# Four products every half unit for the second layer's groups of the last two column blocks, and a new order of GpSimd's steps

## The chip, the cores and the metric

The kernel runs on one core of a Trainium2 chip. A core has five engines that run side by side, each through its own list of instructions in order: TensorE (PE, matrix products into PSUM banks), VectorE (DVE), ScalarE (ACT), GpSimd (POOL, which works in SBUF only) and SyncE (SP), which here issues all DMAs. They wait for each other through semaphores. The metric is the device time of one execution in microseconds (us). Before the change the median of three runs is 1492.81 us (1492.2 to 1493.12).

## The reference

The input is `x`, 2048 rows of 512 in float32. After a layer norm, attention and a two-layer perceptron work on the same normalised rows, and both are added to `x`:

```python
xn = _layernorm(x, axis=-1)
return x + _A_ref(xn, A_wqkv, A_wo) + _B_ref(xn, B_w1, B_b1, B_w2, B_b2)

# _A_ref: 32 heads of 16
scores = jnp.einsum("bhqd,bhkd->bhqk", q, k) * (Dh ** -0.5)
p = _softmax(scores, axis=-1)
o = jnp.einsum("bhqk,bhkd->bhqd", p, v)      # then @ wo

# _B_ref: 512 -> 1792 -> 512
h = _gelu(jnp.einsum("bsd,df->bsf", x, w1) + b1)
return jnp.einsum("bsf,fd->bsd", h, w2) + b2
```

## The kernel before, in words

**Split numbers.** Most products are made from float16 halves. A float32 operand is split into a high part and a low part, and a product of two operands is made of three products (high-high, high-low, low-high; `PAIRS`). The splitting of weights, of projected queries and keys and of gelu outputs is GpSimd's main work: scale or copy to float16 (`hi`), subtract (`lo`).

**Units.** Attention sets the beat. Heads are taken four at a time (8 groups), queries in 4 column blocks of 512, keys in 16 blocks of 128: 8 x 4 x 16 = 512 units. `unit` (one call per unit) writes the instructions of one unit. For four heads it makes scores for the row maxima (`s_half`, PSUM banks "S", reduced by VectorE at L348), and 19 units later (`LEAD`) the transposed scores (`e_half`, banks "T"), whose exponential ScalarE takes (L395); one or two units after that come the products with the values (`v_half`, bank "V"). A unit has two halves (`a` = 0 and 1). In each half the V products use one half of the array's rows and the dense work (below) the other half. A column block of a group of heads is called `t` (32 of them, 16 units each). After its last unit, `v_end` copies the sums and, over the next ten or so units, small steps divide by the softmax sum and store the result `ot` to DRAM; then `t` is `ready`.

**The dense stream.** All other products are groups of a generator: `group(gen)` takes the next one, `dense` writes its products. A group has an order of products, a PSUM bank, a `finish` (the eviction and what follows), perhaps a condition `ready` for each product, and a `pace`: how many products each half of a unit may write. `FAST` is 4 in every unit, `MEAN` 3 and 4 in turn, `SLOW` 3. If a group ends in the middle of a unit's allowance, the rest of the allowance is not used by the next group; if the next product isn't ready, or the generator has nothing (it yields None), the unit passes without. Three generators follow one another:

- `rest`: the last projections of values, queries and keys, 12 products a group, FAST. `project`'s `finish` copies the sum to `pf` on ScalarE (L584, two buffers) and gives two GpSimd steps to `pooled` that write `stg` (L585, L586, three buffers); the DMA to `qk_d` is issued some units later. Beside it `prepare` splits 16 chunks of the layers' weights (`split_steps`, L1173 to L1175), one every 4.5 units. This stage ends when both are through.
- `mlp`: four column blocks `b`. In each, 14 groups of 12 products for the hidden columns (SLOW and FAST in turn; eviction `hh`, L1287; gelu on GpSimd and ScalarE), and then four groups of 42 products for the second layer (MEAN; eviction `yt`, L1310). A product of the second layer needs the gelu of its hidden column to be written out (`done`).
- `tail`: the output projection, 16 groups of 12 products for column blocks 2, 0, 3, 1 in this order. Blocks 2 and 3 begin without the last group of heads, whose part comes in short groups (`o_end`, L526; from `ol` for block 2, from the last `ot` for block 3). A block's groups come only when its read (`read_o`, L1335) has been issued; that is done by `when`, for blocks with `ready`, at places 4 to 13 of every 16 units or after the last score unit. After the last score unit the "S" banks take a second group at two products a half (`spare`), and evictions go to VectorE (L1344); before, to ScalarE and GpSimd (`ys`, L1351). What is left after the last unit is written by `land` and `drain`.

**Order on the queues.** The order on each engine is that in which the Python code calls the instructions; nothing is reordered. Two lists defer work: `later(n, fn)` runs `fn` n units on (bulk transfers wait in a `lane`, one a unit), and `pooled(...)` appends GpSimd steps, each with an assumed time; `run_steps` takes steps from the front at the end of each unit, up to 2500 ns of them.

**Weight chunks.** `chunk` asks for a chunk's two half loads through the lane (`half`, L791); `fetch` asks for one chunk more than the one wanted. `prepare` gives a chunk's split to `pooled` as soon as both halves have been issued (`got[1]`), the split before is through the list, and all values are projected (`got`, `chunk` and the wait at L1207).

Of the kernel before, what the change touches and what calls it, by code (L numbers as in the profile page):

```python
# [24 lines left out]
NT = S // P  # L25
# [7 lines left out]
FAST, MEAN, SLOW = (4, 4), (3, 4), (3, 3)  # L33
# [20 lines left out]
def layer_kernel(ctx: ExitStack, tc: tile.TileContext, x, wqkv, wo, w1, b1, w2, b2, out):  # L54
# [225 lines left out]
    def later(n, fn, local=False, bulk=False):  # L280
        queue.append((slot[0] + n, fn, local, bulk))
# [14 lines left out]

    steps, room = [], [0]

    def pooled(*todo):
        steps.extend(todo)  # L300

    def run_steps(all_of_them=False):
        room[0] = min(room[0], 0) + POOL_NS
        while steps and (room[0] > 0 or all_of_them):
            ns, fn = steps.pop(0)
            room[0] -= ns
            fn()

# [258 lines left out]
    def project(m, w, sb, wh, bank):  # L567

        prods = [lambda c=c, i=i, j=j: (wh[:, w, i, c, :], xt[:, j, c, sb * QB:(sb + 1) * QB])
                 for c in range(NC) for i, j in PAIRS]  # L570

        dst = qk_d[w, m * P:(m + 1) * P, :, sb * QB:(sb + 1) * QB]

        def finish(pj):
            def put():
                nc.sync.dma_start(dst[:, w:w + 2, :], stg)
                nc.sync.dma_start(dst[:, 2 - 2 * w, :], stg[:, 0])
                if not m:
                    later(2, lambda: stacks(0, w, [sb]), True)

            stg = ph.tile([P, 2, QB], F16, name="stg", bufs=3)
            given("act", 600)
            pf = ph.tile([P, QB], F32, name="pf", bufs=2)
            nc.scalar.activation(pf, pj, AF.Copy)  # L584
            hi = lambda: nc.gpsimd.tensor_scalar(stg[:, 0], pf, 1.0, 0.0, op0=ALU.mult, op1=ALU.add)  # L585
            lo = lambda: nc.gpsimd.tensor_tensor(stg[:, 1], pf, stg[:, 0], op=ALU.subtract)  # L586
            later(1, lambda: pooled((620, hi), (1160, lo), (0, lambda: later(2, put, True))), True)

        return Group(prods, bank, finish)

# [22 lines left out]
    pos, spent, cur = [0], [False], [None]  # L613
    v_done = []
# [162 lines left out]
    with ExitStack() as st1:  # L777
# [6 lines left out]
        def chunk(src):  # L784
            wf = ph.tile([P, 4 * W], F32, name="wch", bufs=3)
            v = wf.rearrange("p (a b) -> p a b", b=src.shape[2])
            n = src.shape[1] // 2
            got = [v, 0]

            def half(r):  # L790
                nc.sync.dma_start(v[:, r], src[:, r])  # L791
                got[1] += 1

            for a in range(2):
                later(2, lambda r=slice(n * a, n * a + n): half(r), True, True)
            return got
# [232 lines left out]
        for w in (1, 0):  # L1029
            wf, hi, lo, i1 = ("wq", 0, w), wqh[:, w, 0], wqh[:, w, 1], inv0[:, w:w + 1]  # L1030
# [18 lines left out]
        for i in range(2):  # L1049
            hi, lo = (wvh[j][:, :, i * W:(i + 1) * W] for j in range(2))  # L1050
# [5 lines left out]
            else:  # L1056
                b = add("POOL", 1240, lambda key=key: nc.gpsimd.tensor_scalar(
                    tl[key], tl[key], inv_v[:, 0:1], 0.0, op0=ALU.mult, op1=ALU.add), [h])
# [34 lines left out]
        def turn_m():  # L1093
            tl[mkey] = sb_tile(mkey)
            for k in range(2):
# [7 lines left out]
        put = [add("SP", 600, lambda k=k: nc.sync.dma_start(m_d[0, :, :, 64 * k:64 * k + 64], mhl[32 * k:32 * k + 16]), [a], size=4)  # L1103
               for k in range(2)]
# [73 lines left out]
        def prepare():  # L1178
            am = am_all
            nc.vector.tensor_reduce(am[:, 7:8], b1_s, axis=AX.X, op=ALU.max, apply_absolute_value=True)  # L1180
            nc.vector.tensor_reduce(am[:, 8:9], amx[:, 7:14], axis=AX.X, op=ALU.max)
            nc.vector.tensor_reduce(am[:, 9:10], amx[:, 14:16], axis=AX.X, op=ALU.max)
            box = []
            yield
            yield from scales(am, 14, sbank, box)
            inv, fac = box
            fac1.append(fac)
            inv1.append(inv)
            by_slots(split_qk(1, wfs[1], inv, ready_w))
            nc.vector.tensor_tensor(sexp[:, 1:3], fac[:, 10:14:2], fac[:, 11:14:2], op=ALU.mult)  # L1190
            nc.vector.tensor_scalar_mul(sexp[:, 1:3], sexp[:, 1:3], DH ** -0.5)
            nc.vector.tensor_copy(sexp[:, 3:4], sexp[:, 2:3])
            yield

            nc.vector.reduce_max(gs[:, 0:1], fac[:, 0:8], axis=AX.X)
            nc.gpsimd.tensor_tensor(gs[:, 3:4], fac_v[0][:, 0:1], fac[:, 9:10], op=ALU.mult)
            yield
            nc.vector.reciprocal(gs[:, 1:2], gs[:, 0:1])
            nc.gpsimd.tensor_tensor(gs[:, 2:3], gs[:, 0:1], fac[:, 8:9], op=ALU.mult)
            yield  # L1200
            nc.vector.tensor_scalar_mul(gs[:, 1:2], gs[:, 1:2], 0.5)
            ended = [True]
            for n in range(16):
                while pos[0] < LEAD + WFROM + WSTEP * n:
                    yield
                got = fetch(NM + n)
                while not ended[0] or len(v_done) < NT or got[1] < 2:  # L1207
                    yield
                v = got[0]
                ended[0] = False  # L1210

                def then(wh=None, n=n):
                    ended[0] = True
                    later(2, lambda: put(wh, n), True)

                def put(wh, n):
                    for a in range(2):
                        if n < 7:
                            later(0, lambda a=a: nc.sync.dma_start(w1_d[n, :, a], wh[:, a]), True, True)
                        elif n < 14:  # L1220
                            later(0, lambda a=a: nc.sync.dma_start(w2_d[:, :, 2 * n - 14 + a], wh[:, :, a]), True, True)

                if n >= 14:
                    i = 2 * (n - 14)
                    split_steps(wo_s[:, 0, i:i + 2, :], wo_s[:, 1, i:i + 2, :], v, inv[:, 9:10], then)
                    continue
                if n < 7:

                    wh = ph.tile([P, 2, 2, NC, P], F16, name="wsp", bufs=3)
                    split_steps(wh[:, :, 0], wh[:, :, 1], v.rearrange("p c (a n) -> p a c n", n=P), inv[:, n:n + 1],  # L1230
                                lambda wh=wh, then=then: then(wh))
                else:
                    wh = ph.tile([P, 2, 2, D], F16, name="wsp", bufs=3)
                    split_steps(wh[:, 0], wh[:, 1], v, inv[:, 8:9], lambda wh=wh, then=then: then(wh))
            while not ended[0]:
                yield
# [9 lines left out]
    def mlp():  # L1246
# [3 lines left out]
        done = set()  # L1250
# [21 lines left out]
        for b in range(NQB):  # L1272
# [20 lines left out]
            for q in range(4):  # L1293
# [14 lines left out]
                def store(yp, xa=xa, t=t):  # L1308
# [6 lines left out]

                yield Group([lambda f=f, i=i, j=j, q=q, g=g: (g[:, i, f, q * P:(q + 1) * P], w2_s[:, j, f, :])
                             for f in range(NF) for i, j in PAIRS], dbank, store,
                            lambda n, b=b: (b, n // 3) in done, pace=MEAN)

    def when(t, fn, n=1):  # L1320

# [148 lines left out]
```

## Time and profile before

| | |
|---|---|
| median of three runs | 1492.81 us |
| the profiled execution's own time | 1491.85 us |
| its span, first to last instruction | 1489.9 us |
| TensorE busy, granted clock | 1471.6 us, 0.998 |
| VectorE, ScalarE, GpSimd busy | 1376.0, 1264.9, 660.9 us |
| row maxima (L348), exponentials (L395) | 1296.7 and 1111.4 us |
| last second-layer eviction `yt` | at 1378.3 us |

A row of the profile names the line, the engine, the operation, the tiles (written <- read) with their shapes, a count, and behind the bar the busy time, the mean of one in ns, and the idle time of the engine just before these instructions with what ended it. Timeline rows begin with start and duration in us; square brackets hold the idle time before and its releaser. A row with "x4" is four merged instructions. A busy TensorE isn't TensorE at its peak, since its instructions overlap: four quarter-width instructions (64*32) and both row halves run at the same time. Releasers are inferred.

### The profile page before, as it was taken

To read this page: it belongs to the slowest core of one execution; us is meant where nothing else is said; L and a number is where in the kernel's file an instruction comes from. 1 tells how busy PE (TensorE), PEld (TensorE's weight loads), DVE (VectorE), ACT (ScalarE), POOL (GpSimd) and SP (SyncE) were. 2 spreads that over 40 slices of the span, in tenths; PEclk is the share of its full clock that TensorE was granted. 3 is DMA by queue.
4 is the path that set the end of the run, shared out by engine and by line. 5 is a ranking of instruction groups with operands and counts; after the bars stand their busy time and mean duration, and the time that the engine had idled before them with its cause. 6 is when DMAs were issued, how large, how long until landed. Compare 5 with 4: busy or idle time off the path is not lost.

```text
span 1489.9 us, 88034 instructions
## 1 busy us (share of the span) xinstructions
PE 1471.6 (99%) x40140; PEld 815.1 (55%) x40140; DVE 1376.0 (92%) x2307; ACT 1264.9 (85%) x2365; POOL 660.9 (44%) x671
## 2 busy tenths in 40 slices
PE   8999999999999999999999999999999999999998
PEld 4445555555555555555555555555555555555553
DVE  7899989999999999999999999999999999999913
ACT  5868888888999888899988889998888999888873
POOL 3202667663777311377831137782113777211200
PEclk9999999999999999999999999999999999999999
DMA  7732565553224210211112111121113110111342
GB/s 213 233 104 67 157 194 171 173 177 115 78 70 114 65 37 23 75 54 41 43 44 86 29 46 42 50 71 56 30 30 93 38 43 23 48 53 33 110 131 91
DMA packets 112621, 124.80 MB, mean 84 GB/s; under 512 B 22908, under 2 KB 84220, under 8 KB 112248
## 3 DMA queue, kind: packets, MB, share of 16 engines
q1 hardware_dynamic: 112248, 119.18, 26.6%
q8 instruction: 313, 5.13, 1.5%
q14 instruction: 60, 0.49, 0.1%
HBM read 81.66 MB, written 37.34 MB: 80 GB/s over the span
## 4 chain that ended last, share of the span: by engine, by line
PE 88%; DVE 8%; DMA 2%; ACT 1%; issue 1%; SPq 1%; POOL 0%; DVEq 0%; POOLq 0%; ACTq 0%
PE pV L168 26%; PE pD L168 24%; PE pS L168 18%; PE pT L168 18%; DVE mt L348 6%; PE pT L971 1%; DMA wq<-in_A_wqkv_dram 1%; DVE ac L1344 0%; PE pD L971 0%; DMA qk_d<-stg 0%; DMA kst<-qk_d 0%; DMA qst<-qk_d 0%; DMA m_d<-mhl 0%; ACT xs L924 0%; DVE mneg L364 0%
## 5 line engine op out<-in xcount | busy, mean ns | idle before, releaser
L348 DVE TENSOR_REDUCE mt<-pS 128x1 f32<-128x512 f32 x2029 | 1296.7, 684 | 44.9 <-PE pS L168 26.0
L395 ACT ACTIVATE pe<-pT 128x512 f32<-128x512 f32 x2048 | 1111.4, 599 | 170.2 <-PE pS L168 68.8
L168 PE MATMUL pV<-pe,vv 64*32 64x512 f32 x8192 | 1072.9, 595 | 0.1
L168 PE MATMUL pT<-qst,kst 64*32 64x512 f16 x8192 | 712.9, 377 | 1.8 <-ACT pf L584 1.4
L168 PE MATMUL pS<-kst,qst 62*32 62x512 f16 x8116 | 613.7, 378 | 3.8 <-DVE mt L348 2.2
L168 PEld LDWEIGHTS <-qst 62*32 62x32 f16 x8192 | 278.2, 92 | 221.4 <-issue 52.0
L168 PEld LDWEIGHTS <-kst 64*32 64x32 f16 x8192 | 279.9, 91 | 174.2 <-issue 80.6
L168 PE MATMUL pD<-xb,wc 64*32 64x512 f16 x5376 | 361.4, 377 | 0.0
L168 PE MATMUL pD<-w_s,g 64*32 64x512 f16 x5376 | 359.1, 377 | 0.0
L168 PEld LDWEIGHTS pV<-pe,vv 64*32 64x32 f32 x8192 | 181.5, 105 | 86.0 <-PE pV L168 2.4
L168 PE MATMUL pD<-xt,wqk_h 64*32 64x512 f16 x2400 | 157.6, 378 | 0.0
L168 PEld LDWEIGHTS <-wc 64*32 64x32 f16 x5376 | 116.9, 91 | 43.1 <-issue 0.8
L168 PEld LDWEIGHTS <-g 64*32 64x32 f16 x5376 | 112.9, 91 | 44.2
L1312 POOL TENSOR_TENSOR xa<-xa,yt 128x512 f32<-128x512 f32 x16 | 20.4, 1278 | 242.1 <-ACT yt L1310 242.1
L451 POOL TENSOR_TENSOR osb<-osb,rb 128x512 f32<-128x512 f32 x31 | 39.8, 1284 | 155.3 <-DMA rb<-den_d 126.9
L1267 POOL TENSOR_TENSOR t<-hh 128x512 f32<-128x512 f32 x56 | 58.2, 1040 | 91.8 <-ACT hh L1287 91.0
L1269 POOL TENSOR_TENSOR t<-t,hh 128x512 f32<-128x512 f32 x56 | 71.8, 1282 | 4.7
L1262 POOL TENSOR_TENSOR t<-t,hh 128x512 f32<-128x512 f32 x56 | 71.8, 1282 | 4.7
L1261 POOL TENSOR_SCALAR t<-t,gs 128x512 f32<-128x512 f32 x56 | 38.7, 691 | 65.2 <-ACT t L1256 65.2
L1264 POOL TENSOR_TENSOR g<-t,g 128x512 f16<-128x512 f32 x56 | 65.2, 1164 | 4.7
L168 PEld LDWEIGHTS <-wqk_h 64*32 64x32 f16 x2400 | 54.7, 92 | 19.8 <-issue 0.8
L1173 POOL TENSOR_SCALAR wch<-wch,inv 128x1024 f32<-128x1024 f32 x16 | 17.9, 1119 | 75.3 <-DMA wch<-in_B_w_dram 53.0
(158 smaller groups left out, 911.4 us busy)
## 6 DMA issues: line engine op xcount, KB each, us to landing
wc<-w_d SPq DMA_DIRECT2D x56, 256.0 KB
qk_d<-stg SPq DMA_DIRECT2D x32, 256.0 KB
rb<-den_d SPq DMA_DIRECT2D x124, 64.0 KB
wch<-in_B_w_dram SPq DMA_DIRECT2D x14, 512.0 KB
wch<-in_B_w_dram SPq DMA_DIRECT2D x28, 256.0 KB
w_d<-wsp SPq DMA_DIRECT2D x28, 256.0 KB
kst<-qk_d SPq DMA_DIRECT2D x64, 96.0 KB
qst<-qk_d SPq DMA_DIRECT2D x64, 96.0 KB
```

Source lines behind the costliest of these rows:

```text
L168: p = nc.tensor.matmul(*args, **kw)
L348: nc.vector.reduce_max(mt_of[t][:, n, qt, kb:kb + 1], s, axis=AX.X)
L395: nc.scalar.activation(pe, st, AF.Exp, scale=scale_of[g // 2])
L451: pooled((1280, lambda: nc.gpsimd.tensor_tensor(osb, osb, rb, op=ALU.mult)), (620, lambda: nc.gpsimd.tensor_scalar(ot[:, 0], osb, 1.0, 0.0 ...
L971: nc.tensor.matmul(tl[key], lhs, rhs, start=c + n == 0, stop=(c, n) == (NC - 1, 2))
L1173: pooled((1240, lambda: nc.gpsimd.tensor_scalar(src, src, inv, 0.0, op0=ALU.mult, op1=ALU.add)), (1240, lambda: nc.gpsimd.tensor_scalar(hi ...
L1261: pooled((690, lambda: nc.gpsimd.tensor_scalar(t1, t1, 1.0, gs[:, 1:2], op0=ALU.add, op1=ALU.mult)), (1280, lambda: nc.gpsimd.tensor_tenso ...
L1262: (1280, lambda: nc.gpsimd.tensor_tensor(t1, t1, hh, op=ALU.mult)),
L1264: (1160, lambda: nc.gpsimd.tensor_tensor(g[:, 1, f, :], t1, g[:, 0, f, :], op=ALU.subtract)),
L1267: pooled((1040, lambda: nc.gpsimd.tensor_tensor(t1, hh, hh, op=ALU.mult)), (620, lambda: nc.gpsimd.tensor_scalar(t1, t1, 1.0, 1.0 / GELU_A ...
L1269: (1280, lambda: nc.gpsimd.tensor_tensor(t1, t1, hh, op=ALU.mult)),
L1312: add = lambda: nc.gpsimd.tensor_tensor(xa, xa, yt, op=ALU.add)
```

## The change

Three things are changed.

1. The second-layer groups of blocks 2 and 3 have pace FAST instead of MEAN; those of blocks 0 and 1 keep MEAN.
2. `pooled` has an argument `first`. Steps given with it are inserted in front of all steps that were given without it (behind other such steps). Only `project` uses it, so the conversion of a projection to `stg` goes ahead of weight splits and of the steps for `ot` that wait in the list.
3. A chunk keeps the unit at which its latest half load was issued, plus two, in `got[2]`; `prepare` gives its split to `pooled` no earlier than that.

```diff
-    def pooled(*todo):
-        steps.extend(todo)
+    def pooled(*todo, first=False):
+        n = sum(q[2] for q in steps) if first else len(steps)
+        steps[n:n] = [(*q, first) for q in todo]
 
     def run_steps(all_of_them=False):
         room[0] = min(room[0], 0) + POOL_NS
         while steps and (room[0] > 0 or all_of_them):
-            ns, fn = steps.pop(0)
+            ns, fn, _ = steps.pop(0)
...
-            later(1, lambda: pooled((620, hi), (1160, lo), (0, lambda: later(2, put, True))), True)
+            later(1, lambda: pooled((620, hi), (1160, lo), (0, lambda: later(2, put, True)), first=True), True)
...
-            got = [v, 0]
+            got = [v, 0, 0]
 
             def half(r):
                 nc.sync.dma_start(v[:, r], src[:, r])
                 got[1] += 1
+                got[2] = pos[0] + 2
...
-                while not ended[0] or len(v_done) < NT or got[1] < 2:
+                while not ended[0] or len(v_done) < NT or got[1] < 2 or pos[0] < got[2]:
                     yield
...
-                            lambda n, b=b: (b, n // 3) in done, pace=MEAN)
+                            lambda n, b=b: (b, n // 3) in done, pace=FAST if b > 1 else MEAN)
```

## The prediction

> **What bounds the kernel now.** I read the page first, for the busy shares and the chain that ended last; then stage by stage, since the change touches only some stages.
>
> ```profile
> span 1489.9 us, 88034 instructions
> PE 1471.6 (99%) x40140; PEld 815.1 (55%) x40140; DVE 1376.0 (92%) x2307; ACT 1264.9 (85%) x2365; POOL 660.9 (44%) x671
> PE 88%; DVE 8%; DMA 2%; ACT 1%; issue 1%; SPq 1%; POOL 0%; DVEq 0%; POOLq 0%; ACTq 0%
> L395 ACT ACTIVATE pe<-pT 128x512 f32<-128x512 f32 x2048 | 1111.4, 599 | 170.2 <-PE pS L168 68.8
> ```
>
> TensorE carries the chain, VectorE stands close behind. The 2048 exponentials are four per unit, so there are 512 units, and that number does not change. What the change can move is the length of a unit, stalls inside units, and the work left after the last unit. The stages, by the windows view (second-layer groups at the mean pace; projections at four products; after the last unit):
>
> ```profile
> core 0: us, PE busy (x) PEld busy (x) DVE busy (x) ACT busy (x) POOL busy (x), PEclk, DMA share, GB/s
> 1283.70:1347.20 63.50, 63.33 (x1844) 35.64 (x1836) 62.26 (x104) 53.84 (x101) 11.13 (x10) 1.00 0.19 55
> 279.80:327.90 48.10, 48.06 (x1434) 27.66 (x1418) 46.08 (x76) 40.97 (x79) 33.33 (x30) 1.00 0.57 177
> 1472.30:1489.90 17.60, 12.25 (x160) 5.33 (x156) 9.01 (x14) 0.59 (x1) 0.00 (x0) 0.96 0.45 171
> ```
>
> In the first two, TensorE and VectorE are both full (62.26 of 63.50 us for VectorE). In the last, 17.6 us, nobody exponentiates any more: it is pure tail, and TensorE is at work for 12.25 us of it.
>
> **Part 1: four products per half unit in blocks 2 and 3.** A second-layer group has 14 x 3 = 42 products. At 3 and 4 in turn that is 12 units exactly; at 4 it is ten units of four and one of two, so 11, not 10.5. Eight groups (two blocks of four) give back 8 units of the dense stream, each worth four products.
>
> *Price of a unit.* Starts of exponentials, from ScalarE's timeline, first in a second-layer stage, then among projections (four products always):
>
> ```profile
> 1035.01 2.30 ACT L395 ACTIVATE pe<-pT 128x512 f32<-128x512 f32 x4 [0.59 <-PE pS L168]
> 1037.59 2.32 ACT L395 ACTIVATE pe<-pT 128x512 f32<-128x512 f32 x4 [0.28 <-PE pS L168]
> 1040.20 2.30 ACT L395 ACTIVATE pe<-pT 128x512 f32<-128x512 f32 x4 [0.29 <-PE pT L168]
> 1042.78 1.09 ACT L395 ACTIVATE pe<-pT 128x512 f32<-128x512 f32 x2 [0.28 <-PE pS L168]
> 313.69 1.09 ACT L395 ACTIVATE pe<-pT 128x512 f32<-128x512 f32 x2 [0.26 <-PE pT L168]
> 316.33 1.09 ACT L395 ACTIVATE pe<-pT 128x512 f32<-128x512 f32 x2 [0.30 <-PE pT L168]
> 318.94 1.09 ACT L395 ACTIVATE pe<-pT 128x512 f32<-128x512 f32 x2 [0.28 <-PE pT L168]
> L1310 ACT ACTIVATE yt<-pD,gs x4: 691/691/692, 1283.0 to 1378.3; 128x512 f32<-128x512 f32 x4
> L584 ACT ACTIVATE pf<-pD x12: 605/605/606, 254.7 to 344.3; 128x512 f32<-128x512 f32 x12
> ```
>
> Units alternate 2.58 and 2.61 us at the mean pace (mean 2.595); with four products throughout they take 2.64 and 2.61 (2.625). So a unit pays 0.03 us; 80 full units pay 2.4, the eight units of two products nothing. The reason that it is so little: the dense products run on one half of the array's rows while the V products run on the other.
>
> ```profile
> 1461.50 0.63 PE L168 MATMUL pV<-pe,vv 64*32 64x512 f32 x4
> 1461.67 0.61 PE L168 MATMUL pD<-wo_s,oc 64*32 64x512 f16 x8
> 1461.96 0.61 PE L168 MATMUL pV<-pe,vv 64*32 64x512 f32 x4
> 1462.10 0.61 PE L168 MATMUL pD<-wo_s,oc 64*32 64x512 f16 x8
> ```
>
> Eight V instructions end at 1462.57, the sixteen of four dense products at 1462.71: four just fit beside them. The Trainium skill, page "TensorEngine Tiling (Array Packing)", section Key Properties, says that tiles operate independently and load and multiply in parallel; taken strictly the fourth product would be free, this term 0 instead of 2.4 and the sum -9.7 instead of -7.3. The starts above say nearly so, not quite, and I keep 2.4.
> The bounds: 0 below; above, the whole difference of the stages, (344.3 - 254.7) / 33 units = 2.715 against (1378.3 - 1283.0) / 36 = 2.647, or 0.068 x 88 = 6.0 us. Most of that difference belongs to group ends (one eviction per 3 units against one per 12), hence the value near the bottom.
>
> The 8 units won become output-projection units, with an eviction every 3 units: 8 x 0.068 = 0.5 us.
>
> *Inputs.* Their GpSimd work must keep up: with the faster pace, the last hidden column's products come in the tenth unit of a group rather than the twelfth; hidden and gelu work is not touched. If the last column is a unit late, its three remaining products still fit in the eleventh unit.
>
> *The tail.* After the last unit (TensorE, ScalarE and VectorE timelines):
>
> ```profile
> 1471.26 0.60 ACT L421 ACTIVATE osb<-pV 128x512 f32<-128x512 f32 x1 [4.32 <-issue]
> 1472.36 0.66 PE L473 MATMUL pS<-ident,osb 128*128 128x128 f32 x4
> 1474.45 1.91 PE L168 MATMUL pS<-wo_s,oc 64*32 64x512 f16 x60
> 1475.23 0.68 DVE L482 TENSOR_TENSOR ot<-pS,ot 64x512 f16<-64x512 f32 x1 [1.46 <-ACT ot L481]
> 1476.48 3.91 PE L168 MATMUL pD<-wo_s,oc 64*32 64x512 f16 x64
> 1480.32 2.76 PE L526 MATMUL pD<-wo_l,ol 64*128 64x512 f16 x12
> 1480.43 6.15 DVE L1344 SCALAR_TENSOR_TENSOR ac<-pD,gs,ac 128x512 f32<-128x512 f32 x9 [2.48 <-PE pD L168]
> 1482.92 2.75 PE L526 MATMUL pD<-wo_l,ot 64*128 64x512 f16 x12
> ```
>
> The last block's own input `ot` is ready at 1475.91, but its twelve matmuls start at 1482.92, behind left-over work: 60 + 64 quarter instructions (124 / 4 = 31 half products, 15.5 whole) and twelve for `ol`, 27.5 products in all. The 8 units bring 32 products forward, so all of it can be gone. Then `ot`'s matmuls start at 1475.9, the first group is there 2.75 / 4 = 0.69 later, and four evictions at 6.15 / 9 = 0.68 follow: 1479.3. Today the last eviction ends at 1486.58 and the span 3.3 us later. Gain 7.3 us. Bounds: 7.7 (the transposes at 1472.36 could start 0.4 us earlier without the products before them); 4.6, if the four `ol` evictions still stand ahead on VectorE (4 x 0.68).
> Who could be late: column block 0's attention output, used from 1412.0, its read issued at 1386.67 by SP; `ol`, issued at 1453.38.
>
> ```profile
> L168 PE MATMUL pD<-wo_s,oc x744: 372/376/388, 1412.0 to 1480.0; 64*32 64x512 f16 x186
> 1386.67 2.54 SPq L1335 DMA_DIRECT2D oc<-ot_d  x4
> 1453.38 0.55 SPq L1416 DMA_DIRECT2D ol<-ot_d  x1
> ```
>
> The use moves 8 units, 21 us, to about 1391. The read is programmed four units after the tail's start but only at places 4 to 13 of 16: by the code's count it can move 4 units (10.6 us), to about 1376 to 1380. Ten us remain for it. `ol` would be used about 1465, 12 us after its issue.
>
> **Part 2: GpSimd's order.** Among the projections GpSimd stands in a weight split whose load has not landed, and projections queue behind it (GpSimd, ScalarE and SP timelines):
>
> ```profile
> 185.82 0.48 SPq L791 DMA_DIRECT2D wch<-in_B_w_dram  x1
> 191.38 1.12 POOL L1173 TENSOR_SCALAR wch<-wch,inv 128x1024 f32<-128x1024 f32 x1 [13.64 <-DMA qst<-qk_d]
> 196.52 1.15 POOL L586 TENSOR_TENSOR stg<-pf,stg 128x512 f16<-128x512 f32 x1
> 197.70 0.60 ACT L584 ACTIVATE pf<-pD 128x512 f32<-128x512 f32 x1 [2.57 <-POOL stg L586]
> POOL stg L586: 3.4, 2
> ```
>
> GpSimd idles 13.64 us, three projections pile up on two `pf` buffers, and ScalarE, with the exponentials behind, stops for 2.57 us (the row names another DMA as releaser; the split's second half load had been issued at 185.82). Two such stops make 3.4 us; some 0.3 us before such a pair is usual (rows above), so 2.9 is lost. With the split two units later and projections ahead of it, the first of the three is converted before GpSimd waits, and two buffers suffice: I take -2.9. Bounds: 0, if the stop just moves, and -3.4. The cover: if a load lands later than two units after its issue (here 5.6 us against 5.3) GpSimd still waits, with at most one projection behind it. On SP, the stores of split weights go two units later, past other transfers; the first layer reads them many units on.
>
> **Sum** against the profiled execution: -2.9 + 2.4 + 0.5 - 7.3 = -7.3, from 1491.85 (span 1489.9) to 1484.55. The median shown, 1492.81, is 0.96 above it: 1485.5. Corners: -3.4 + 0 - 7.7 = -11.1 (1481.7) and 0 + 6.0 + 0.5 - 4.6 = +1.9 (1494.7).
>
> **Rivals.**
> *The stream outruns block 0.* If its read keeps its old place, the 8 units pass without products and the tail keeps its 27.5: -2.9 + 2.4 = -0.5, 1492.3. For it: the read has fixed places. Against: `t=28` is ready some units before, by the code. 0.10.
> *The GpSimd stop moves elsewhere.* No -2.9: -4.4, 1488.4. For it: landing in 5.6 us. 0.12.
> *Four products cost the stages' whole difference.* +6.0 for 2.4: -3.7, 1489.1. Against: the alternation 2.58 and 2.61. 0.12.
> *The clock drops in the thinned tail.* The row 1472.30:1489.90 already has 0.96 with TensorE busy 12.25 of 17.6 us; with 8.6 us of products taken out before `ot` (1.91 + 3.91 + 2.76) it stands idle between the transposes. At half clock the last twelve take 5.5 instead of 2.75 and bound the evictions: 1475.9 + 5.5 + 0.7 = 1482.1 for 1479.3, +2.8 (the sum -4.5), 1488.3. The page "TensorE: Matmul & The Clock Gate" of the Trainium skill, section "What's actually happening", states half rate after an idle window of about 3.4 us; in this trace only the 0.96 points there. 0.11.
> *Slower: weight splits outlast the projections.* The first stage ends only when both are through.
>
> ```profile
> L1173 POOL TENSOR_SCALAR wch<-wch,inv x16: 1109/1118/1126, 143.1 to 323.0; 128x1024 f32<-128x1024 f32 x16
> ```
>
> Sixteen splits, 179.9 / 15 = 12.0 us apart, which is the 4.5 units that the code sets. If each became two units (5.3 us) longer, the last would start at 402, 58 us after the last projection (344.3): some 22 units without products; less the 8 won, 14 units or 56 products fall into the tail at 2.76 / 12 = 0.23 us: 12.9 - 2.9 + 2.9 = +12.9, 1505.7. It decides from about a unit per split on (16, less 8 units of slack between 323 and 344.3, less 8 won). Against: loads are asked for a split ahead, so that the two units fall into the 4.5. 0.08.
>
> **How the numbers follow.** Forecast 0.47, rivals as given. A measurement here tells about 0.2% (3 us) from no change. Faster: forecast, moved stop, clock, and 0.07 of the fourth-product case: 0.77; same: block 0 and the other 0.05: 0.15; slower: 0.08. The range 1482.0 to 1490.5 holds the forecast's own (1482 to 1488) and the cases at 1488.3, 1488.4 and 1489.1; 0.18 stay outside.
>
> **What would show it.** `yt` in the last two blocks 11 units apart, some 29.1 us instead of 31.8; the last `yt` about 21 us earlier and two more `ys`; no `oc` or `ol` products after the transposes of the last block, and `ot` matmuls right behind L482; ScalarE never waiting for L586. I am wrong if TensorE waits for `oc` about 1391, if units without products stand before it, if units in those blocks take 2.7 us, or if the first layer starts later than the 91st unit or so.

## The result and the profile after

The changed kernel takes 1497.81 us (median of seven runs, 1496.43 to 1501.0) against 1492.81 for the kernel before (1491.7 to 1494.75): a ratio of 1.0034 [1.0023, 1.0046]. It is slower by 5 us. The forecast was 1485.5.

The profiled execution of the changed kernel took 1501.0 us, 3.2 above its median; that of the kernel before took 1491.85, 1.0 below its own. The traces therefore differ by more (9.3 us of span) than the medians do.

From the page of the changed kernel, the span, the busy times and the group of the transposed scores; behind it that group's row from the page before:

```profile
span 1499.2 us, 88105 instructions
...
PE 1471.7 (98%) x40176; PEld 810.4 (54%) x40176; DVE 1375.4 (92%) x2304; ACT 1266.8 (84%) x2367; POOL 663.7 (44%) x673
...
L168 PE MATMUL pT<-qst,kst 64*32 64x512 f16 x8192 | 710.6, 378 | 7.7 <-ACT ys L1353 3.7
```

```profile
L168 PE MATMUL pT<-qst,kst 64*32 64x512 f16 x8192 | 712.9, 377 | 1.8 <-ACT pf L584 1.4
```

TensorE's busy time is the same as before (1471.7 against 1471.6), so the time does not come from more work. The last row of the first view names a wait (behind the second bar: idle before these instructions, 7.7 us, and what ended most of it): TensorE waited 3.7 us for a `ys`. Before, the same group had 1.8 us of idle time, mostly behind a `pf`.

To see where the two traces part I took the start of every fourth exponential, which is the start of a unit (units 0 to 511), and subtracted one trace from the other by stretch of units (us, changed minus before):

| stretch | units | difference |
|---|---|---|
| up to the first exponential | | +1.4 |
| projections and weight splits | 0 to 95 | +3.1 |
| hidden columns, blocks 0 and 1 | 96 to 333 | +0.2 |
| blocks 2 and 3 with the new pace | 334 to 470 | +3.9 |
| the stage's end, the first `ys` | 470 to 480 | +6.2 |
| output projection | 480 to 494 | +3.0 |
| last units | 494 to 511 | 0.0 |
| after the last exponential | | -8.4 |

The tail gained what was forecast and more: from the start of the last unit's exponentials to the end it is 25.3 us before and 16.9 after. The losses stand elsewhere, and the largest is at the place where the second layer's stage ends. The chain of waits of the changed kernel in the stretch 1355 to 1410 (start, length, what; the pieces around the stop):

```profile
1373.45 1.17 POOL ot L454
1374.63 0.56 SPq L459
1375.24 0.59 SPq L459
1376.00 4.51 issue
1380.51 0.70 ACT ys L1353
1381.25 0.40 PE pT L168 x4
```

The transposed scores (`pT`) hang on a `ys`, the `ys` on 4.51 us named "issue", and ahead of these stand SP's writes of `ot` (L459 here, L458 before) and the division that makes `ot`. The `ys` itself has no operand that was late. SP's timeline there, changed kernel, and then the kernel before:

```profile
1374.63 2.46 SPq L459 DMA_DIRECT2D ot_d<-ot  x4
1377.14 1.62 SPq L1315 DMA_DIRECT2D acc_d<-xa  x1
```

```profile
1365.89 3.25 SPq L458 DMA_DIRECT2D ot_d<-ot  x4
...
1380.39 0.34 SPq L1313 DMA_DIRECT2D acc_d<-xa  x1
```

In both, the second layer's last store, `acc_d<-xa`, follows the `ot` writes of column block 28. Before, the `ot` writes had gone at 1365.89, well ahead of the stage's end, and the store had 8 us until the first `ys`. In the changed kernel the stage ends at unit 471, while block 28's division is still under way; the end of the stage writes out all deferred steps at once (`flush`), so the store stands on SP behind writes whose data GpSimd finishes at 1374.6. It is issued at 1377.14, though its own data had been ready since 1367.75 (GpSimd's timeline):

```profile
1366.47 1.28 POOL L1314 TENSOR_TENSOR xa<-xa,yt 128x512 f32<-128x512 f32 x1 [26.91 <-ACT yt L1312]
```

The groups of `ys`, changed kernel, then before:

```profile
L1353 ACT ACTIVATE ys<-pD,gs x6: 687/692/692, 1380.5 to 1425.4; 128x512 f32<-128x512 f32 x6
L1353 ACTq EVENT_SEMAPHORE  x3: 17/38/5315, 1375.0 to 1375.1; - x3
  issue: 4.5, 1
```

```profile
L1351 ACT ACTIVATE ys<-pD,gs x4: 691/691/692, 1388.5 to 1413.1; 128x512 f32<-128x512 f32 x4
L1351 ACTq EVENT_SEMAPHORE  x3: 38/38/38, 1387.7 to 1387.8; - x3
```

One semaphore wait ahead of the first `ys` took 5315 ns; before, all three took 38. `ys` lies in the third stage's pool (`ph3`), which takes over the memory of the second's (`ph2`), and my reading is that this memory is free only when the last store out of it has landed. The trace has the store's burst of transfers end at about 1380.0, and the `ys` starts at 1380.51. ScalarE's exponentials stand in line behind it.

The stop itself makes 4.5 of the 6.2 us (unit 475); another 1.65 fall in the unit behind it, where TensorE's granted clock is halved. The stop and the 3.3 us that follow it, by windows (columns as in the prediction; PEclk is the third from the end):

```profile
1377.10:1381.50 4.40, 0.67 (x20) 0.12 (x8) 0.97 (x2) 0.99 (x2) 0.22 (x1) 1.00 0.23 75
1381.60:1384.90 3.30, 3.30 (x64) 2.09 (x63) 1.06 (x2) 1.86 (x5) 0.95 (x1) 0.50 0.00 0
```

The reading of the stop at the `ys` rests on inferred waits, and runs had to show it. Three smaller places stand beside the stop: stops of TensorE, mostly named "issue", among the projections (units 26, 50, 71 and 85, +4.2 in all; the expectations below call units 0 to 95 the first layer, though the first layer's products come behind them), one at unit 482 (2.6 us of TensorE's time), and ScalarE's stop for GpSimd, which is gone as forecast (unit 36: -2.28, unit 51: -0.53).

### The profile page after: what moved, and what is told of

It reads as the page before. It is cut to its first block, busy times and chain, and to the rows that moved or that the text cites. A ratio compares the mean times of both kernels' runs of the same rounds, so it can differ in the third digit from the quotient of the medians.

```text
span 1499.2 us, 88105 instructions
## 1 busy us (share of the span) xinstructions
PE 1471.7 (98%) x40176; PEld 810.4 (54%) x40176; DVE 1375.4 (92%) x2304; ACT 1266.8 (84%) x2367; POOL 663.7 (44%) x673
## 4 chain that ended last, share of the span: by engine, by line
PE 87%; DVE 7%; DMA 2%; ACT 1%; issue 1%; SPq 1%; POOL 0%; POOLq 0%; ACTq 0%; DVEq 0%
PE pV L168 25%; PE pD L168 24%; PE pS L168 18%; PE pT L168 17%; DVE mt L349 6%; PE pT L973 2%; DMA wq<-in_A_wqkv_dram 1%; PE pD L973 1%; DMA rb<-den_d 0%; SPq L459 0%; DMA m_d<-mhl 0%; PE pT L943 0%; SPq L1337 0%; DMA den_d<-dn 0%; DVE ac L1346 0%
## 5 line engine op out<-in xcount | busy, mean ns | idle before, releaser
L168 PEld LDWEIGHTS <-qst 62*32 62x32 f16 x8192 | 282.5, 92 | 240.5 <-issue 59.0
L168 PEld LDWEIGHTS <-kst 64*32 64x32 f16 x8192 | 271.9, 91 | 168.7 <-issue 77.0
L168 PE MATMUL pD<-wo_s,oc 64*32 64x512 f16 x840 | 55.1, 378 | 0.0
```

The costliest lines, as they stand in the source:

```text
L168: p = nc.tensor.matmul(*args, **kw)
```

## The experiments

**First: which part loses?** Theory A puts the loss into the pace, by way of the stage's early end; theory B into GpSimd's order. The three edits were run apart, on one chip, with the kernel before.

The pace alone:

```diff
-                            lambda n, b=b: (b, n // 3) in done, pace=MEAN)
+                            lambda n, b=b: (b, n // 3) in done, pace=FAST if b > 1 else MEAN)
```

> Only the pace is changed; GpSimd's order and the splits' wait are as before. Theory A (the early end of the second stage costs): the end of the stage, 8 units earlier, falls into the division steps of the block t=28. SP then stands at the stores of ot, the last store of xa to acc_d comes after them, and the first ys of the output projection waits for its landing: about 6 us lost at units 475 and 476, and about 3 us more some six units on. The units of the last two blocks take 2 to 2.5 us more, the tail after the last exponential 8 us less, and a stop of 1.4 us at unit 498 goes: sum about +2, 1494 to 1496. Rival B (all of the loss is GpSimd's new order): no stop at unit 475, about -6, 1486 to 1488.

GpSimd's part alone (`first`, and the two units more; all groups MEAN):

```diff
-    def pooled(*todo):
-        steps.extend(todo)
+    def pooled(*todo, first=False):
+        n = sum(q[2] for q in steps) if first else len(steps)
+        steps[n:n] = [(*q, first) for q in todo]
...
-                while not ended[0] or len(v_done) < NT or got[1] < 2:
+                while not ended[0] or len(v_done) < NT or got[1] < 2 or pos[0] < got[2]:
```

> GpSimd's order and the two units' wait as in the changed kernel, pace as before. If what the two traces show holds (the stops of ScalarE at units 36 and 51 gone, -2.8; new stops of TensorE near units 26, 50, 60, 71 and 85, +5.8): +1.5 to +4.5, 1494 to 1497, all of it before unit 96, and from there on every unit as long as before. Rival (my forecast was right, and the new stops were that execution's own): -2 to -3, 1490.

And each half of that part by itself, `first` without the added wait, and the added wait without `first`:

> Only projections ahead of splits; splits go to GpSimd as soon as both half loads are issued. If the projections' place is what removes the stops at units 36 and 51, and the wait is what adds the new ones: about -2.5, 1490. If the order alone shifts the stores so that TensorE stops elsewhere: 1493 to 1496. If a projection still comes behind a split that waits for its load (the split of unit 30 is written before the projections of units 33 and 36): no change, 1492.5 to 1493.5, with the stop at unit 36 as before.

> Only the two units' wait; projections in the order in which they come. If the wait adds the new stops: the stops near units 26, 50 to 62, 71 and 85 as in the changed kernel, 1494 to 1497. If the stops come from the order: about -2, since the split of unit 30 now goes behind the projection of unit 30 and the stop at unit 36 is gone, 1490 to 1491.

Measured against the kernel before: the pace alone 1.0036 [1.0022, 1.0049]; GpSimd's part 1.0013 [1.0000, 1.0026]; `first` alone 1.0000 [0.9988, 1.0012]; the wait alone 1.0005 [0.9993, 1.0017]. The pace carries the whole loss of the change; it lost more than the 1494 to 1496 us expected for it (median 1497.89). Its trace shows the same order on SP and the same stop (SP's timeline, then a row each of ScalarE's and TensorE's, pace alone):

```profile
1371.60 2.47 SPq L458 DMA_DIRECT2D ot_d<-ot  x4
1374.11 1.35 SPq L1313 DMA_DIRECT2D acc_d<-xa  x1
```

```profile
1377.23 0.69 ACT L1351 ACTIVATE ys<-pD,gs 128x512 f32<-128x512 f32 x1 [4.48 <-issue]
```

```profile
1377.96 0.61 PE L168 MATMUL pT<-qst,kst 64*32 64x512 f16 x4 [3.69 <-ACT ys L1351]
```

GpSimd's part doesn't lose that much, but by itself it doesn't gain either. It is taken up again below.

**Second: is it the store, and the memory it gives back?** Four kernels, again on one chip. The first leaves block 2 at the old pace, so that the stage ends four units later (unit 475) and block 28's division is through:

```diff
-                            lambda n, b=b: (b, n // 3) in done, pace=MEAN)
+                            lambda n, b=b: (b, n // 3) in done, pace=FAST if b > 2 else MEAN)
```

> Only block 3 has four products; GpSimd as before. The second stage then ends 4 units earlier, at unit 475, when the block t=28 is through its division. Theory A (what costs is that the end of the stage meets that division): no stop at units 475 and 476, units +1.0 us, half of the tail's products gone (about 16 of 27.5, at 0.23 us: -3.7): 1488 to 1490.5. Rival C (the stage's end itself costs, wherever it falls: the first ys must wait for the last store of acc_d in any case): a stop of several us at the new end too, 1494 or more.

The second keeps the pace of the change and puts only the last residual store three units earlier, so that on SP it goes ahead of the `ot` writes:

```diff
-                    later(1, lambda: pooled((1280, add), (0, lambda: later(4, put, True))), True)
+                    later(1, lambda: pooled((1280, add), (0, lambda: later(1 if t == NT - 1 else 4, put, True))), True)
```

> The pace as changed, and the last store of xa to acc_d is put three units earlier, ahead of the stores of ot on SP. Theory A: it is issued about 9 us earlier (near 1366 instead of 1375), the stop of ys (4.5 us, 6.7 us of unit time at units 475 and 476) is gone: some 6 less than the pace alone, about 1491.5. If ys waits for something else (the division of t=28, a product): no change, 1497 to 1498. The stop at unit 482 may stay (theory D, below) or go with the first.

The third keeps the store where it is and gives `ys` other memory, that of the pool which lives through both stages (with one buffer for two); the order of the instructions on every engine is that of the pace alone:

```diff
-        ys = p3[0].tile([P, D], F32, name="ys", bufs=2)
+        ys = feed[0].tile([P, D], F32, name="ys", bufs=1)
```

> The pace as changed, and ys lies in memory that the second stage did not use (one buffer); every engine's order is the same as with the pace alone. If ys waits only because its memory is handed over when the last store of the stage has landed: no stop of ScalarE at ys, unit times at 475 and 476 as before, about 6 less than the pace alone, 1491 to 1492. If it is the product or the bank that is late: no change, 1497 to 1498.

The fourth is the second with the reads of blocks 3 and 1 asked for later, to test theory D (the stop at unit 482 comes of many bulk reads at once):

```diff
-                fetch(qb, (2, 4, 10, 16)[n])
+                fetch(qb, (2, 4, 18, 20)[n])
```

> As the kernel with the earlier store, and the reads of column blocks 3 and 1 come later (18 and 20 units after the tail's start instead of 10 and 16), so that the read of block 0 stands alone. Theory D (the stop of 2.6 to 3.1 us at unit 482, in which TensorE waits for nothing that the profile shows, is a late load of its instructions behind the bulk reads bunched on the DMA queues): the stop shrinks to under 1 us, 1 to 3 us less than with the earlier store alone. If it has nothing to do with the transfers: it stays.

Measured, ratio to the kernel before on the same chip (the pace alone ran on another chip than the rest) and difference of the stretch from unit 470 to 480 in one trace of each:

| kernel | ratio | 470 to 480 |
|---|---|---|
| pace alone (from above) | 1.0036 [1.0022, 1.0049] | +6.8 |
| block 3 alone | 0.9977 [0.9966, 0.9988] | +0.2 |
| earlier store | 0.9992 [0.9979, 1.0005] | +0.4 |
| `ys` in other memory | 0.9990 [0.9978, 1.0001] | +0.4 |
| earlier store, later reads | 1.0045 [1.0032, 1.0057] | +0.4 |

The stop is gone in all four. With block 3 alone the store still goes behind the `ot` writes, but at 1373.59, 8.5 us ahead of the first `ys`. SP's timeline with the earlier store, and the row of ScalarE's:

```profile
1362.59 0.37 SPq L1313 DMA_DIRECT2D acc_d<-xa  x1
1369.02 2.46 SPq L458 DMA_DIRECT2D ot_d<-ot  x4
```

```profile
1370.16 0.69 ACT L1351 ACTIVATE ys<-pD,gs 128x512 f32<-128x512 f32 x1
```

The store goes 7.6 us ahead of the first `ys`, and that has no idle time before it. With `ys` in other memory SP's order is as bad as ever, and it does no harm: the `ys` starts without idle time before it, 1.3 us before the store is even issued (SP's timeline, then ScalarE's):

```profile
1372.21 2.48 SPq L458 DMA_DIRECT2D ot_d<-ot  x4
1374.73 1.21 SPq L1313 DMA_DIRECT2D acc_d<-xa  x1
```

```profile
1373.41 0.69 ACT L1351 ACTIVATE ys<-pD,gs 128x512 f32<-128x512 f32 x1
```

So two things had to come together, the store behind the `ot` writes on SP and the memory that it hands over; taking away either takes away the stop. Theory A is shown.

The kernel with later reads missed its expectation. The stop around unit 482 was gone, but TensorE then waited for the read that had been moved (TensorE's and SP's timelines):

```profile
1427.87 0.62 PE L168 MATMUL pS<-wo_s,oc 64*32 64x512 f16 x4 [4.88 <-DMA oc<-ot_d]
```

```profile
1419.31 3.16 SPq L1335 DMA_DIRECT2D oc<-ot_d  x4
...
1423.15 2.58 SPq L1335 DMA_DIRECT2D oc<-ot_d  x4
```

The two moved reads were issued from 1419 to 1426, and the first group of the "S" banks, which is block 3's, wanted its rows at 1423. This is what the prediction's rival "The stream outruns block 0" described, at another block and made by hand: block 3's read, asked for eight units later, comes too late for a stream that starts eight units earlier.

**Third: what is left of the change, and what it could be.** The whole change with the earlier store; six quick groups (block 3 and the last two of block 2) with the earlier store, GpSimd as before; and the kernel with pace and earlier store, with block 1's read alone asked for later; all on one chip. (Two of the expectations speak of half units; `later` counts whole units, so the store goes three units earlier and the read is asked for four later.)

```diff
-                    later(1, lambda: pooled((1280, add), (0, lambda: later(4, put, True))), True)
+                    later(1, lambda: pooled((1280, add), (0, lambda: later(1 if t == NT - 1 else 4, put, True))), True)
```

> The whole change (pace, first, longer wait), and the last residual rows' store put three half units earlier, so that on SP it stands ahead of block 28's output writes. Theory A (the first ys waits for memory that the late store of the residual rows hands over, worth 6.2 us between units 470 and 480): that stretch falls from +6.21 us to under +1, and the time from 1.0034 of before to 0.998 to 1.001, since the first layer's losses (some +1 to +3 us) and the later stop about unit 482 (+1.5 to +3) stay. Rival: the full change loses for a reason of its own, the pace and GpSimd's new order together, and the time stays above 1.0025 of before although the stop at the ys is gone.

```diff
-                            lambda n, b=b: (b, n // 3) in done, pace=MEAN)
+                            lambda n, b=b: (b, n // 3) in done, pace=FAST if b > 2 or b == 2 and q > 1 else MEAN)
```

> The quick pace for block 3's four groups and the last two of block 2 (six groups instead of eight), with the earlier store; GpSimd as before. The stream should end about unit 473. Theory A with the fix: no stop at the ys, the tail some 5.2 to 6.8 us shorter, the price of the units +1.5 to +2, and so 0.9970 to 0.9990 of before, between the runs with block 3 alone (0.9977) and with both blocks and the earlier store (0.9992). If theory D holds (the stop behind units 480 to 486 comes from how many bulk reads fall together with the reload of TensorE's instructions), whether that stop of 1.4 to 3 us appears here is what decides between the two ends: with it 0.999, without it 0.997.

```diff
-                fetch(qb, (2, 4, 10, 16)[n])
+                fetch(qb, (2, 4, 10, 20)[n])
```

> Quick pace for both blocks, earlier store, and only block 1's read of attention rows and of residual rows asked for four half units later (20 instead of 16); block 3's read is not moved, so no product should wait for it. Theory D (TensorE's stop about unit 484, +1.4 us beside the earlier store alone, comes where the read of block 1 falls together with those of block 3 and of the residual rows): the stretch from 480 to 494 falls from +1.57 us to under +0.5 and the time from 0.9992 to about 0.998. Rival: these stops fall where they fall, by the place of TensorE's instruction loads alone, and a stop of 1 to 3 us shows at some other unit from 480 to 500, the time staying 0.999 to 1.0005.

The whole change with the earlier store: 0.9989 [0.9980, 0.9997]. From 1.0034 that is 0.45%, 6.7 us, for one store three units earlier; the stretch from 470 to 480 fell from +6.2 to +0.4. Six quick groups: 0.9969 [0.9954, 0.9983]. Block 1's read asked for later: 0.9984 [0.9975, 0.9994], and in its trace the stop at unit 482 is there all the same, with the clock at 0.50 for 3.4 us behind it (TensorE's timeline, first the changed kernel, then this one):

```profile
1404.02 0.40 PE L168 MATMUL pT<-qst,kst 64*32 64x512 f16 x4 [2.60 <-issue]
```

```profile
1395.03 0.61 PE L168 MATMUL pT<-qst,kst 64*32 64x512 f16 x4 [2.37 <-issue]
```

This run says nothing on theory D, for its edit doesn't reach the stop. Block 1's read is issued at unit 491 with the earlier store and at unit 492 here, some 25 us behind the stop; only its residual rows moved, from units 488 to 491 to units 495 and 496 (SP's timeline, earlier store, then this kernel):

```profile
1416.63 2.60 SPq L1335 DMA_DIRECT2D oc<-ot_d  x4
```

```profile
1422.71 3.60 SPq L1335 DMA_DIRECT2D oc<-ot_d  x4
```

Up to the stop both kernels are the same code, so its absence in one trace and presence in the other show that it comes and goes with the execution (or the chip, as the two ran on different ones); the one profiled here (1494.9 us) is the slowest of twelve, 5.7 us above their median. What bears on theory D is the kernel with later reads, in which block 3's read moved from unit 481 to 492 and the stop at 482 is absent. But the whole change with the earlier store has no such stop either (+0.4 in units 480 to 494), with the reads left where they are. Theory D is neither shown nor refuted.

**Fourth: the two best parts together,** six quick groups, the earlier store and GpSimd's new order:

> The quick pace for six groups (block 3 and the last two of block 2) with the earlier store, and now GpSimd's new order with its longer wait as well. If GpSimd's part is worth what the prediction gave it (2.9 us), the time goes from 0.9969 of before (six groups without it) to about 0.995. If its gain is given back to TensorE's stops for instructions, as the runs with that part alone say (1.0000 to 1.0013 of before), it stays at 0.9965 to 0.998. In the profile ScalarE should not wait for L587, and the sum of TensorE's stops named issue in the first layer (18.4 us with six groups, 22 to 25 in most runs of the new order, 18.9 in the full change with the earlier store) says whether the gain is kept in that execution.

1485.13 us (five runs), 0.9948 [0.9933, 0.9963]: by this ratio 7.8 us faster than the kernel before on its chip, the best of all. That is the 0.995 expected if GpSimd's part were worth 2.9 us: it adds 0.21% here, with intervals that overlap (0.9954 to 0.9983 without it, 0.9933 to 0.9963 with it), on two chips, each against its own runs of the kernel before. Two other pairs with and without the part show nothing: 1.0034 against 1.0036 for the change and the pace alone, 0.9989 against 0.9992 with the earlier store.

**GpSimd's part over all traces.** The stop of ScalarE for `stg`, 3.4 us before, is absent from every trace with GpSimd's part or half of it (six), and present in every trace of the old order (eight). But in the old order it isn't always 3.4: in the waits from 95 to 365 us, which hold most of units 0 to 95, it is 3.4, 3.4, 2.8, 2.8, 2.6, 2.2 and 2.0, and with six quick groups and the old order, whose code is that of before up to there, this (us in total, times, longest):

```profile
ACT pf L584 <- POOL stg L586: 0.2, 1, 0.2
```

And TensorE's stops named "issue" come and go with the execution. The same waits in the changed kernel and then in the same with the earlier store, which are the same code too up to there:

```profile
PEld L168 <- issue: 25.5, 73, 2.1
PE pS L168 <- issue: 1.8, 2, 1.4
```

```profile
PEld L168 <- issue: 18.9, 65, 1.7
```

In neither does ScalarE wait for `stg`. Yet units 0 to 95 took 3.1 us more than before in the first execution and 2.0 us less in the second. Over all traces, units 0 to 95 took 0.9 us more than in the trace of before in the mean of eight with the old order (that trace itself among them, as 0; from -1.0 to +2.4) and 1.0 us more in the mean of six with the new one (from -2.0 to +3.1). So the stop that I saw is removed and nothing can be seen of it in the mean.

## Why the prediction was wrong

**"Who could be late" is the step that failed.** The tail was pulled forward by eight units, and I asked of two reads, block 0's and `ol`'s, whether they would be in time. They were: the first matmul with `oc`, at 1408.19 in the changed kernel (unit 483, eight units earlier than before), has no idle time ahead of it. I did not ask the same of the output projection's other inputs: the memory in which its first eviction `ys` is written, and the instructions on SP that give it free. The trace before showed the two that mattered, `acc_d<-xa` at 1380.39 and the first `ys` at 1388.5, and how little lay between them: 8 us, where the `ys` was to move 21 us earlier. The store moved too, but not with it, as it stands behind block 28's division, which has its own time. This cost 6.2 us in the trace, and 6.7 between the whole change with and without the earlier store. None of the signs I gave of being wrong named it, and neither did a rival: the nearest, the stream that outruns block 0's read, is the same mechanism, an input with a fixed place, with the wrong input.

**The tail, -7.3, came out, in part by luck.** `yt` in the last two blocks, changed kernel:

```profile
1305.82 0.69 ACT L1312 ACTIVATE yt<-pD,gs 128x512 f32<-128x512 f32 x1
1336.29 0.69 ACT L1312 ACTIVATE yt<-pD,gs 128x512 f32<-128x512 f32 x1
1365.64 0.69 ACT L1312 ACTIVATE yt<-pD,gs 128x512 f32<-128x512 f32 x1
```

The last two are 29.35 us apart (29.1 forecast; between the pair before lies unit 454, 1.25 us longer than in the trace of before), and there are six `ys` for four, as said. The last `yt` is eight units earlier, but 12.7 us and not 21, since the units ahead of it had lost 8.6 us in this trace. The end, TensorE's timeline of the changed kernel, then VectorE's:

```profile
1490.39 0.63 PE L480 MATMUL pS<-ident,on 128*64 128x128 f32 x4 [0.81 <-DVE on L477]
1491.70 0.60 PE L527 MATMUL pD<-wo_l,ot 64*128 64x512 f16 x2 [0.68 <-ACT ot L482]
1492.48 2.82 PE L527 MATMUL pD<-wo_l,ot 64*128 64x512 f16 x10 [0.17 <-DVE ot L483]
```

```profile
1491.74 0.68 DVE L483 TENSOR_TENSOR ot<-pS,ot 64x512 f16<-64x512 f32 x1 [1.40 <-ACT ot L482]
1492.90 2.07 DVE L1346 SCALAR_TENSOR_TENSOR ac<-pD,gs,ac 128x512 f32<-128x512 f32 x3 [0.48 <-PE pD L527]
1495.33 0.75 DVE L1346 SCALAR_TENSOR_TENSOR ac<-pD,gs,ac 128x512 f32<-128x512 f32 x1 [0.36 <-PE pD L527]
```

No `oc` or `ol` products stand after the transposes, and the `ot` matmuls come right behind the addition (L483 here), as forecast. From that addition's end to the last eviction's it is 3.66 us for my 3.4 (10.67 before), a gain of 7.0; another 1.2 us of the 8.4 lie ahead of it, where fewer products stand between the last exponential and the transposes. With the pace and no stop at the `ys`, the tail is 6.7 to 6.8 us shorter in the other traces of eight quick groups, 5.5 and 6.1 with six and 5.2 with four. That this is near 7.3 is luck: the 1.2 us, which the sum didn't have, make up for most of what the clock takes.

**The clock rival came true in most traces.** Why 6.7 and not 8.4: the tail of the whole change with the earlier store by windows, and its last matmuls:

```profile
1473.90:1476.90 3.00, 1.42 (x12) 0.78 (x8) 1.49 (x4) 0.60 (x1) 0.00 (x0) 1.00 0.70 262
...
1477.90:1482.90 5.00, 5.00 (x12) 1.39 (x10) 2.70 (x4) 0.00 (x0) 0.00 (x0) 0.50 0.27 105
```

```profile
1477.63 5.30 PE L527 MATMUL pD<-wo_l,ot 64*128 64x512 f16 x12 [0.68 <-ACT ot L482]
```

The clock falls to 0.50 and the twelve matmuls take 5.30 us for 2.75, close to the rival's 5.5; the last eviction ends 5.4 us after the addition instead of 3.4, so the price is 2.0 us and not the rival's 2.8. Over the last 17.6 us of the span the clock was 0.96 before, and 0.72 to 0.80 in eight of the nine later traces in which the pace was changed; the ninth, block 3 alone, has 0.91. In the profiled execution of the change (0.86) the clock fell too, but at 1494.2, behind most of the last matmuls; the mean clock of that execution is 0.995 and that of its six others 0.992 to 0.994. The Trainium skill, page "TensorE: Matmul & The Clock Gate", section "What's actually happening", puts half rate after an idle window of about 3.4 us; here TensorE was busy for 1.42 of the 3 us before the drop and nowhere idle for a whole microsecond, so a thinned stretch is enough. I had given this 0.11 and as an alternative; in the five traces with eight quick groups and no stop at the `ys` it is a term of the sum, some +2 at the last matmuls.

**The price of a unit was right.** First and last unit of the stretch with the new pace, before and then with the pace and the earlier store:

```profile
992.64 1.09 ACT L395 ACTIVATE pe<-pT 128x512 f32<-128x512 f32 x2 [0.60 <-PE pS L168]
1353.56 2.30 ACT L395 ACTIVATE pe<-pT 128x512 f32<-128x512 f32 x4 [0.29 <-PE pT L168]
```

```profile
992.79 1.08 ACT L395 ACTIVATE pe<-pT 128x512 f32<-128x512 f32 x2 [0.59 <-PE pS L168]
1356.40 1.77 ACT L395 ACTIVATE pe<-pT 128x512 f32<-128x512 f32 x3 [0.30 <-PE pT L168]
```

360.92 against 363.61 us, +2.7, and +0.4 more from unit 470 to 480: 3.1 for the 2.4 + 0.5 of the sum. The first stretch costs 2.7 in three traces of eight quick groups and 3.5 to 4.1 in the four others, the changed kernel's among them; in those unit 454 alone is 0.7 to 1.5 us longer, and the rest is 2.6 to 2.7 again. The rival that priced four products at the whole stage difference falls, and so does a free fourth product.

**Part 2's -2.9 is the second term that failed.** The step was right about the mechanism (the stop at unit 36 goes with either half of the edit) and wrong to take one execution's stop for a gain of the kernel. The rival "moves elsewhere" is the nearest, but it isn't moved by the edit: TensorE's stops named "issue" are there with both orders and vary by some us. The measured effects of the part lie between -0.21% (with six quick groups, where it is all that was forecast) and +0.13% (by itself). That it gains a little is possible and not shown. The slower rival, weight splits that outlast the projections, did not happen: units 96 to 333 cost +0.2.

**What the sum would have been.** -7.3 + 6.2 (the `ys` stop) + 2.9 (no gain in Part 2) + 3.0 (units 480 to 494, mostly the stop at 482) is +4.8, and the medians differ by 5.0. That it closes so well is luck: the clock's 2 us are not in it, since they are missing in the profiled execution, and its last term is from one execution, the slowest of seven, and isn't explained; with the pace and no stop at the `ys` it was +0.4 to +1.6 in three traces and +4.3 in the one with block 1's read asked for later.

**Why six groups beat eight.** With GpSimd's new order and the earlier store, six have 0.9948 [0.9933, 0.9963] and eight 0.9989 [0.9980, 0.9997], on two chips; with the old order the intervals overlap (0.9969 [0.9954, 0.9983] against 0.9992 [0.9979, 1.0005]). By the traces, two groups more cost 1.05 us in units 334 to 470 (2.69 against 1.64, earlier store against six groups), 0.4 at the stage's end, 0.6 in units 480 to 494 and 1.2 in the last units, and bring 1.4 in the tail (6.84 against 5.45), in one trace of each. The tail has less to give than the stretches before it take. One part shows in all executions, the clock: its mean is 0.997 or more in nearly all executions of the kernel before, 0.996 at most in the 35 of the three kernels with eight groups, the earlier store and no late read of block 3, and 0.997 or more in six of the 12 with six groups. These six took 1483.2 to 1485.1 us, the other six 1485.9 to 1489.1. What else makes the difference is not shown. What the last units wait for is not followed up either; near unit 495 TensorE waits for rows of `qst` (2.4 us with `ys` in other memory, 0.8 in the whole change with the earlier store).

**Open.** What makes TensorE stop at some units (26, 50, 71, 482 to 486, 498) in some executions. Where it does, the trace has two loads of its instructions 6 to 7 us apart where some 4.5 is usual (1394.4 and 1401.1 ahead of the stop at 1404.02), and bulk transfers running meanwhile (the DMA view of the changed kernel, 1394.40 to 1402.40 in 40 slices, busy tenths):

```profile
DMA  5666996778999989999999999999999999999999
```

But loads as far apart stand at other places without a stop. Only the kernel with later reads moves a transfer ahead of unit 482, and one trace without the stop is not enough, since another without it has the transfers in place. No run here takes the transfers away altogether.

## What to carry to other kernels

When work is pulled forward, list everything its first instruction needs: operands, and also the memory it writes, who hands that over, and what stands ahead of the handing-over instruction on its queue; the slack in the trace of before, minus the distance moved, is the answer for each. A stop seen in one profiled execution is worth its length only if it is there in most executions: compare stretches of the same code over several traces before putting it into a sum. And of a gain that comes in equal portions, try fewer: here, with one store moved and GpSimd's new order, six of eight portions came to 0.9948 of the time before and all eight to 0.9989, on two chips.

## What the runs showed of the hardware that was not expected

- The granted clock fell to 0.50 after 3 us in which TensorE was busy 47% of the time, with no idle stretch of a whole microsecond; falling ahead of the last matmuls it made twelve of them 5.30 us, falling behind most of them left ten at 2.82. It also fell to 0.50 for 3.4 us behind the 4.5-us stop at the `ys`, which made the stop cost 6.2 us.
- Units 0 to 95 took 264.3 us in the execution profiled before, and from 1.0 us less to 2.4 us more in seven others of the same code; the stops ahead of TensorE's weight loads that the profile can only call "issue" came to 18.4 to 22.8 us in them (95 to 365 us).
